# Score tiles of up to 512 columns in a fused attention and FFN kernel, with a few changed places in its schedule

## Chip, cores and metric

The kernel runs on one core of one Trainium2 chip. The metric is device microseconds for one execution; lower is better. Before the change the median of three runs is 322.86 us (322.22 to 323.26).

## What is computed

Two stages follow each other. The first is attention over 4 batches, 8 heads, 768 tokens and a head size of 64, in which a query sees only the keys that fall to the same one of 16 clusters. The second is a gated feed-forward network (FFN) on the 3072 tokens, with a model width of 512 and an inner width of 1536.

```python
q_assign = argmax(q_n . c_n); k_assign = argmax(k_n . c_n)
scores = where(q_assign == k_assign, q @ k.T / sqrt(64), -1e9)
attn = softmax(scores) @ v                      # per batch and head
x = attn, heads side by side                    # 3072 x 512
out = (sigmoid(x @ w_gate) * (x @ w_val)) @ w_out
```

## The kernel before

**Attention.** A head's 768 queries and 768 keys are six blocks of 128 each. q and k are split into a high and a low half-precision part (`hl`: `sp`, `hi`, `lo` in the schedule), turned by a transposing DMA or by TensorE (`turn`, `tn`, `tu`; L410), and stand then in the tile `T`. From T come the cluster logits (`lg`; L421, L434), from these VectorE picks the best cluster (`pick`, `pk`; L449 to L469), and the picked clusters are turned (`ot`) and put into 16 rows of T (`hop`, `hp`, `pl`), so that the score matmul adds the mask by itself.

**Score steps.** `head_steps` (L859) cuts a pass of one head into steps. A step is one key block j against three query blocks: one score matmul of 128 x 384 (L893, `do_scores`), one exponential on ScalarE into the tile `es` (L898), and later three matmuls of 128 x 65 with v (AV; L916, `do_av`). `sc` takes one of four PSUM banks of a ring that gates, values, logits and some v sums (`vt`, L341) use too. Batch 0 goes in two rounds: all eight heads for the first three query blocks (6 steps each), then all for the last three. In the later batches the heads of pairs 0 to 2 are passes of 36 blocks (12 steps), and the last pair's two heads go in two rounds of 18 blocks (6 steps). AV of a step is issued three steps behind its scores in batch 0, two behind in the later ones (`LA`).

**FFN beside attention.** When the first or second half of a batch's queries is done, `ffn_block` puts the FFN of these tokens on a queue: 12 times four gate matmuls (L530), a tanh on ScalarE (L536), four value matmuls (L546) and a product on VectorE (L551), then the output matmuls (L684 in batch 0; L821 with VectorE's sums L768 in the later ones, which make two token blocks' products out of seven half-size ones; `product_out`, L744). `ffn_run` (L845) hands out pieces of this queue after each score step, as far as a credit goes; the credit grows by `ns` nanoseconds a step, from the table `SCHED` by batch and quarter of the batch (`ns23`: batch 2, last quarter).

**Order of the work.** It is written out by hand. `SCHED` gives each background piece a time in steps, relative to the step in which its pair of heads begins: `b1p3lg1` is the logits of the second head of pair 3 in batch 1. `run_bg` (L958) issues what has come due, once at a half step and once at a step. `step_no` counts steps from 0 to 384. Each engine executes its instructions in the order of issue. The pieces `vs`, `vu`, `vt` make the sum of v (L330, L336 and L337, L341); where a batch has no entry of its own, it takes those that begin with `b2`.

**Ends of a pass.** `normalise` (L366, L370 to L375) divides by the sum and writes xp on GpSimd (POOL); `turn_x` (L938) turns xp into xTb, the FFN's input, by a transposing DMA (L947) or, for some pairs of batch 0, by TensorE (L944).

**Constants.** An identity matrix (`ident`), the centroids (`cen`, `c2`) and their squares (`sq`) have tiles of their own; `wo` holds w_out, whose second half (`wo[1]`) is loaded during batch 0's second round.

Of the kernel before, what the change touches and what calls it, by code (L numbers as in the profile page):

```python
# [8 lines left out]
FP = mybir.dt.float32  # L9
HP = mybir.dt.float16  # L10
# [84 lines left out]
}  # L95


@with_exitstack
def kernel(
# [13 lines left out]
    B, H, S, D = q.shape  # L113
# [4 lines left out]
    NCH = S // 128  # L118
# [42 lines left out]
    def bank(n=512, dt=FP, name="bank"):  # L161
        return ring.tile([128, n], dt, tag="ring", name=name)
# [49 lines left out]

    cen = const.tile([128, D], FP, name="cen")

# [62 lines left out]

    c2 = const.tile([128, 2, D], FP, name="c2")
    sq = const.tile([128, D], FP, name="sq")
    ss = const.tile([128, 1], FP, name="ss")  # L280
# [578 lines left out]
    def head_steps(b, p, e, halves):  # L859
        t = T[b, 2 * p + e]  # L860
        steps = []
        cuts = [PARTS[c] if b == 0 else (3 * c, 3) for c in halves]
        for j in range(NCH):
            for c, (a, n) in zip(halves, cuts):
                steps.append(dict(
                    b=b, p=p, e=e, nq=sum(z for _, z in cuts), k=t[:, j, :], h0=cuts[0][0],
                    h1=c, q=t[:, 6 + a : 6 + a + n, :], j=j, c0=a - cuts[0][0], n=n,
                ))
        steps[0]["first"] = True
        steps[-1]["last"] = True  # L870
        return steps
# [14 lines left out]
    def do_scores(s):  # L886
        ready(s)
        sc = bank(128 * s["n"], name="sc")
# [4 lines left out]
        PE.matmul(  # L893
            out=sc.rearrange("p (c t) -> p c t", t=128), lhsT=s["k"], rhs=s["q"],
            start=True, stop=True,
        )
        es = esp.tile([128, NB], HP, name="es")[:, 0 : 128 * s["n"]]
        ACT.activation(es, sc, AF.Exp, scale=SCALE)  # L898
        s["es"] = es

    def do_av(s):
# [12 lines left out]
        a0 = nq * e if both else 0  # L914
        for i in range(s["n"]):
            PE.matmul(  # L916
                out=av[:, a0 + s["c0"] + i, :], lhsT=s["es"][:, bass.ts(i, 128)],
                rhs=VA[b, p][:, e, s["j"], :],
                start=(first and i == 0 and a0 == 0),
                stop=(last and i == s["n"] - 1 and (e == 1 or not both)), skip_group_check=True,  # L920
            )
# [607 lines left out]
    for b in range(B):  # L1529
        xT = xtp.tile([128, NDC, S], HP, tag="xTb", name="xTb")  # L1530
        key = min(b, 1)
        for i in range(2 if b else NPT):
            u = BASE[b] + (DONE0[i] if b == 0 else 96 - 12 * halved(b) if i == 0 else 96)
            lag = SCHED.get(f"lag{key}{i}", 8)
            if b == B - 1 and i:
                break
            c0, cn = PARTS[i] if b == 0 else (3 * i, 3)
            for w in range(1 + (cn > 3)):
                z = cn // (1 + (cn > 3))
                at(u + lag, lambda xT=xT, b=b, a=c0 + z * w, n=z: ffn_block(xT, 128 * a, 128 * n, b))  # L1540
        for p, e, c in heads(b):
            for s in head_steps(b, p, e, c):
                s["xT"] = xT
                do_scores(s)
                run_bg(step_no[0] - 0.5)
                pend.append(s)
                r = step_no[0] - BASE[b]
                ns = SCHED.get(f"ns{b}{r // 24}", SCHED.get(f"ns{b}", 500.0))
                ns += SCHED.get(f"nx{step_no[0]}", 0)
# [41 lines left out]
```

## Time and profile before

| what | value |
|---|---|
| median of three runs | 322.86 us |
| the profiled execution, whole | 323.67 us |
| its span | 321.9 us |
| instructions | 9181 |
| granted TensorE clock | 0.999 |
| exponentials of scores | 384 of 128 x 384 |
| score matmuls | 384 of 128 x 384 |
| AV matmuls | 1152 of 128 x 65 |
| gate and value matmuls | 384 and 384 of 128 x 384 |

The profile is of one execution. Its engines are PE (TensorE), PEld (its weight loads, which overlap), DVE (VectorE), ACT (ScalarE), POOL (GpSimd) and SP (the queue that issues most DMAs). A row of the timeline gives the start, the duration, the engine, the line, the operation, out<-in, the shapes, the count, and in brackets how long the engine was idle before it and what ended that. Records of matmuls overlap, as the ends are those of the last column's way out; the distance from start to start says how long one takes. A row of the groups gives busy time, mean duration in ns, and the idle time before.

### The profile page before, as it was taken

What the parts mean: (1) busy time and instruction counts of PE and PEld (TensorE: products, weight loads), DVE (VectorE), ACT (ScalarE), POOL (GpSimd) and SP (SyncE); (2) the same over time, 40 slices, a digit from 0 to 9 for tenths busy, and PEclk for the clock granted to TensorE, in tenths of its full rate; (3) what the DMA queues carried; (4) which work ended last, traced back from release to release, by engine and by line L of the source; (5) the groups of instructions that cost most, each with busy time, mean ns of one, the idle gap of its engine ahead of it and who ended that gap; (6) DMA issues with size and microseconds to landing.
All of it is one profiled execution on the core that took longest, in us unless ns stands there. A gap on an engine that the chain in (4) does not pass through costs nothing.

```text
span 321.9 us, 9181 instructions
## 1 busy us (share of the span) xinstructions
PE 314.6 (98%) x3510; PEld 222.4 (69%) x3510; DVE 224.9 (70%) x598; ACT 231.1 (72%) x521; POOL 108.6 (34%) x145
## 2 busy tenths in 40 slices
PE   7999999999999999999999999999999999999996
PEld 5888666766666666666777687566777688667775
DVE  5799656777787677576878587586767356456666
ACT  6688988787888888877867866778877886332320
POOL 6877464154434365433133333414211111000000
PEclk9999999999999999999999999999999999999999
DMA  7999997738876996978884751942503112200103
GB/s 214 374 256 180 244 171 118 210 75 236 238 113 187 163 238 155 223 172 136 108 219 115 217 113 33 314 110 52 111 2 90 40 26 79 77 2 1 65 2 131
DMA packets 77709, 45.16 MB, mean 140 GB/s; under 512 B 56865, under 2 KB 75105, under 8 KB 77665
## 3 DMA queue, kind: packets, MB, share of 16 engines
q1 hardware_dynamic: 73696, 39.73, 49.7%
q0 software_dynamic: 3680, 4.72, 9.0%
q8 instruction: 27, 0.44, 0.6%
q10 hardware_dynamic: 288, 0.13, 0.2%
q14 instruction: 18, 0.14, 0.2%
HBM read 28.34 MB, written 6.29 MB: 108 GB/s over the span
## 4 chain that ended last, share of the span: by engine, by line
PE 89%; DMA 3%; DVE 3%; issue 2%; POOL 1%; SPq 0%; ACT 0%; POOLq 0%; DVEq 0%
PE g L530 19%; PE v L546 19%; PE sc L893 17%; PE av L916 10%; PE o L821 8%; PE o L684 5%; PE lg L434 2%; PE o_end L594 2%; DMA T<-hl 2%; PE lg L421 1%; PE t_ps L1142 1%; PE o L594 1%; DMA xTb<-xp 1%; PE oh_ps L1202 1%; DMA qraw<-in_q_dram 1%
## 5 line engine op out<-in xcount | busy, mean ns | idle before, releaser
L898 ACT ACTIVATE es<-sc 128x384 f16<-128x384 f32 x384 | 174.3, 492 | 40.6 <-PE sc L893 31.9
L893 PE MATMUL sc<-T 128*128 128x384 f16 x384 | 117.8, 326 | 0.4 <-DVE T L1223 0.4
L916 PEld LDWEIGHTS <-es 128*128 128x128 f16 x1152 | 81.3, 98 | 35.9 <-issue 0.8
L916 PE MATMUL av<-va,es 128*128 128x65 f16 x1152 | 97.6, 194 | 0.0
L551 DVE SCALAR_TENSOR_TENSOR hT<-th,v 128x384 f16<-128x384 f32 x96 | 53.0, 553 | 55.6 <-PE av L916 36.0
L530 PE MATMUL g<-xTb,wg 128*128 128x384 f16 x384 | 78.2, 326 | 0.7 <-DMA xTb<-xp 0.5
L546 PE MATMUL v<-xTb,wv 128*128 128x384 f16 x384 | 78.1, 326 | 0.0
L536 ACT ACTIVATE th<-g 128x384 f32<-128x384 f32 x96 | 47.2, 491 | 35.0 <-PE g L530 15.9
L375 POOL TENSOR_TENSOR xp<-t,rec 128x384 f16<-128x384 f32 (+1 forms) x30 | 21.6, 720 | 101.8 <-DVE rec L372 52.3
L530 PEld LDWEIGHTS <-wg 128*128 128x128 f16 x384 | 37.2, 97 | 19.3 <-issue 0.4
L546 PEld LDWEIGHTS <-wv 128*128 128x128 f16 x384 | 37.4, 98 | 18.6
L893 PEld LDWEIGHTS <-T 128*128 128x128 f16 x384 | 37.1, 97 | 0.6 <-DVE T L1223 0.5
L1459 POOL TENSOR_TENSOR hl<-kraw,hl 128x384 f16<-128x384 f32 x22 | 20.2, 920 | 41.1 <-DVE hl L1458 20.5
L1459 POOL TENSOR_TENSOR hl<-qraw,hl 128x384 f16<-128x384 f32 x22 | 20.9, 950 | 9.8 <-DVE hl L1458 9.8
L768 DVE TENSOR_TENSOR ob<-o,ob 128x256 f32<-128x256 f32 (+1 forms) x35 | 17.8, 523 | 7.6 <-PE o L821 6.8
L370 DVE TENSOR_TENSOR t<-av,sv 128x390 f32<-128x390 f32 (+1 forms) x30 | 14.4, 479 | 9.7 <-PE av L916 7.3
L821 PEld LDWEIGHTS <-sum 128*128 128x128 f16 x168 | 16.4, 98 | 5.2 <-issue 0.8
L684 PE MATMUL o<-wo,hT 128*128 128x512 f16 x72 | 19.9, 379 | 0.0
L821 PE MATMUL o<-wo,hT 128*128 128x256 f16 x126 | 19.8, 272 | 0.0
L449 DVE TENSOR_REDUCE lgs<-lg 128x192 f32<-128x384 f32 x23 | 12.7, 551 | 2.8 <-PE lg L434 2.7
L821 PEld LDWEIGHTS <-hT 128*128 128x128 f16 x126 | 12.2, 97 | 3.4
L322 POOL CAST va<-vraw 128x768 f16<-128x768 f32 x15 | 13.0, 869 | 1.9 <-DMA vraw<-in_v_dram 1.9
(158 smaller groups left out, 340.1 us busy)
## 6 DMA issues: line engine op xcount, KB each, us to landing
vraw<-in_v_dram SPq DMA_DIRECT2D x15, 384.0 KB, 4.9
kraw<-in_k_dram SPq DMA_DIRECT2D x14, 384.0 KB, 4.3
qraw<-in_q_dram SPq DMA_DIRECT2D x12, 384.0 KB, 4.2
out_dram<-ob SPq DMA_DIRECT2D x18, 256.0 KB, 2.4
wg<-in_moe_w_gate_dram POOLq DMA_DIRECT2D x2, 768.0 KB, 9.5
wv<-in_moe_w_val_dram POOLq DMA_DIRECT2D x2, 768.0 KB, 10.3
wo<-in_moe_w_out_dram POOLq DMA_DIRECT2D x2, 768.0 KB, 9.3
T<-ohT SPq DMA_DIRECT2D x44, 24.0 KB, 1.9
```

Source lines behind the costliest of these rows:

```text
L375: (eng or POOL).tensor_tensor(x, t[:, 0:nq, 0:64], bcast(rec[:, 0:nq], 64), ALU.mult)
L530: PE.matmul(out=g[:, 0:n], lhsT=wg[fc // WQ][:, dc, fc % WQ, :], rhs=xT[:, dc, t0 : t0 + n], start=(dc == 0), stop=(dc == NDC - 1),)
L536: ACT.activation(th[:, 0:n], g[:, 0:n], AF.Tanh)
L546: PE.matmul(out=w[:, 0:n], lhsT=wv[fc // WQ][:, dc, fc % WQ, :], rhs=xT[:, dc, t0 : t0 + n], start=(dc == 0), stop=(dc == NDC - 1),)
L551: DVE.scalar_tensor_tensor(HB[b, blk][:, fc, 0:n], st[0][:, 0:n], 1.0, w[:, 0:n], ALU.add, ALU.mult)
L684: PE.matmul(out=o, lhsT=HB[b, blk][:, fc, bass.ts(t, 128)], rhs=wo[fc // WON][:, fc % WON, :], start=(fc == 0), stop=(fc == NFC - 1),)
L768: plus = lambda dst, a, z: DVE.tensor_tensor(dst, a, z, ALU.add)
L821: PE.matmul(out=st[z][:, e], lhsT=a[:, c, :], rhs=rhs[:, c, :], start=start and c + e == 0, stop=c == HF - 1, skip_group_check=True,)
L893: PE.matmul(out=sc.rearrange("p (c t) -> p c t", t=128), lhsT=s["k"], rhs=s["q"], start=True, stop=True,)
L898: ACT.activation(es, sc, AF.Exp, scale=SCALE)
L916: PE.matmul(out=av[:, a0 + s["c0"] + i, :], lhsT=s["es"][:, bass.ts(i, 128)], rhs=VA[b, p][:, e, s["j"], :], start=(first and i == 0 and a ...
L1459: POOL.tensor_tensor(hl[:, :, 64:128], r, hl[:, :, 0:64], ALU.subtract)
```

## The change

A step is no longer always three blocks. `head_steps` lists the (key block, query block) units of a pass and cuts them into tiles: in the first round of batch 0 three at a time as before; in a pass of 36 nine tiles of four; in a pass of 18 three tiles of four and two of three. A tile may reach over two key blocks: then `do_scores` issues two score matmuls into the two parts of one bank, and one exponential over the whole. `do_av` issues one AV matmul for each unit. A tile counts d = n/3 steps: `step_no` and the credit of the FFN queue grow by that, so background pieces keep their places in units of work, but are issued at the tiles' grid.

So that the larger `es` tiles fit, `ident`, `cen`, `c2` and `sq` lie in `wo[1]`, before it is loaded.

In the table, `b1p3lg1` goes from -29 to -28, `ns23` from 491 to 410, and five entries are new for batch 3, which took those of `b2` before: `vs` of pair 0 -30 (-19), `vu` -28 (-17), `vt` -9 (2), and `lg0` and `pk0` of pair 1 -32 (both -39). `END` is not read.

```diff
-    "b1p3lg0": -38.0, "b1p3pk0": -36.5, ... "b1p3lg1": -29, "b1p3pk1": -27.0,
+    "b1p3lg0": -38.0, "b1p3pk0": -36.5, ... "b1p3lg1": -28, "b1p3pk1": -27.0,
-    "ns21": 491, "ns22": 481, "ns23": 491, "ns30": 443,
+    "ns21": 491, "ns22": 481, "ns23": 410, "ns30": 443,
+    "b3p0vs": -30, "b3p0vu": -28, "b3p0vt": -9, "b3p1lg0": -32, "b3p1pk0": -32, "END": 0,
...
-    NB = 128 * max([3] + SIZES)
+    NB = 512
...
-    ident = const.tile([128, 128], FP, name="ident")
+    spare = wo[1].rearrange("p a m -> p (a m)").bitcast(FP)
+    ident = spare[:, 0:128]
...
-        for j in range(NCH):
-            for c, (a, n) in zip(halves, cuts):
-                steps.append(dict(... k=t[:, j, :], q=t[:, 6 + a : 6 + a + n, :], j=j, n=n))
+        units = [(j, a + z) for j in range(NCH) for a, n in cuts for z in range(n)]
+        if b == 0 and base["h0"] == 0:
+            sizes = [3] * NCH
+        else:
+            sizes = [4] * 9 if len(units) == 36 else [4, 4, 4, 3, 3]
+        for n in sizes:
+            w = []
+            for j, a in units[:n]:
+                if w and w[-1][0] == j:
+                    w[-1] = (j, w[-1][1], w[-1][2] + 1)
+                else:
+                    w.append((j, a, 1))
+            units = units[n:]
+            steps.append(dict(base, w=w, d=n / 3))
...
-        PE.matmul(out=sc..., lhsT=s["k"], rhs=s["q"], start=True, stop=True)
+        for j, a, n in s["w"]:
+            PE.matmul(
+                out=sc[:, x : x + 128 * n].rearrange("p (c t) -> p c t", t=128),
+                lhsT=s["t"][:, j, :], rhs=s["t"][:, 6 + a : 6 + a + n, :], start=True, stop=True,
+            )
+            x += 128 * n
...
-                step_no[0] += 1
+                u = round(3 * (step_no[0] + s["d"])) / 3
+                step_no[0] = int(u) if u == int(u) else u
```

More of the change, by code (lines that the diff above doesn't have):

```diff
@@ L211, in load @@
         eng.dma_start(out=t, in_=view(side, b, p))
-    cen = const.tile([128, D], FP, name="cen")
+    cen = spare[:, 128 : 128 + D]
     def load_head(eng, side, p, e, c=slice(0, 6)):
@@ L276, in mix_wo @@
         DVE.tensor_tensor(o[:, c], a[:, c], z[:, c], ALU.subtract)
-    c2 = const.tile([128, 2, D], FP, name="c2")
-    sq = const.tile([128, D], FP, name="sq")
+    c2 = spare[:, 256 : 256 + 2 * D].rearrange("p (a d) -> p a d", a=2)
+    sq = spare[:, 512 : 512 + D]
     ss = const.tile([128, 1], FP, name="ss")
@@ L862, in head_steps @@
         cuts = [PARTS[c] if b == 0 else (3 * c, 3) for c in halves]
-        for j in range(NCH):
-            for c, (a, n) in zip(halves, cuts):
[L865 to L868, printed above, removed]
+        base = dict(
+            b=b, p=p, e=e, nq=sum(n for _, n in cuts), h0=cuts[0][0], h1=halves[-1], t=t, d=1.0,
+        )
[13 more added lines that the diff above has]
+            steps.append(dict(base, w=w, d=n / 3))
         steps[0]["first"] = True
@@ L887, in do_scores @@
         ready(s)
-        sc = bank(128 * s["n"], name="sc")
+        N = 128 * sum(n for _, _, n in s["w"])
+        sc = bank(N, name="sc")
         for _ in range(SCHED.get(f"nd{step_no[0]}", 0)):
@@ L892, in do_scores @@
             )
[L893 to L897, printed above, removed]
+        x = 0
+        for j, a, n in s["w"]:
+            PE.matmul(
+                out=sc[:, x : x + 128 * n].rearrange("p (c t) -> p c t", t=128),
+                lhsT=s["t"][:, j, :], rhs=s["t"][:, 6 + a : 6 + a + n, :], start=True, stop=True,
+            )
+            x += 128 * n
+        es = esp.tile([128, NB], HP, name="es")[:, 0:N]
         ACT.activation(es, sc, AF.Exp, scale=SCALE)
@@ L914, in do_av @@
         a0 = nq * e if both else 0
-        for i in range(s["n"]):
+        parts = [(j, a + z - s["h0"]) for j, a, n in s["w"] for z in range(n)]
+        for i, (j, c) in enumerate(parts):
             PE.matmul(
-                out=av[:, a0 + s["c0"] + i, :], lhsT=s["es"][:, bass.ts(i, 128)],
-                rhs=VA[b, p][:, e, s["j"], :],
+                out=av[:, a0 + c, :], lhsT=s["es"][:, bass.ts(i, 128)], rhs=VA[b, p][:, e, j, :],
                 start=(first and i == 0 and a0 == 0),
-                stop=(last and i == s["n"] - 1 and (e == 1 or not both)), skip_group_check=True,
+                stop=(last and i == len(parts) - 1 and (e == 1 or not both)),
+                skip_group_check=True,
             )
@@ L1547 @@
                 r = step_no[0] - BASE[b]
[L1548 to L1549 removed]
+                ns = s["d"] * SCHED.get(f"ns{b}{int(r // 24)}", SCHED.get(f"ns{b}", 500.0))
                 ffn_run(ns if b or r >= DONE0[0] else 0.0)
```

4 rows, old and new, of the table SCHED are left out of this document.

## The prediction

> **What bounds the kernel now.** I read the page's table of engines first, then the costliest groups, then stretches of the timeline for TensorE's own spacing, and last the places where TensorE starts late. Page, engines and two groups:
>
> ```profile
> PE 314.6 (98%) x3510; PEld 222.4 (69%) x3510; DVE 224.9 (70%) x598; ACT 231.1 (72%) x521; POOL 108.6 (34%) x145
> ...
> L898 ACT ACTIVATE es<-sc 128x384 f16<-128x384 f32 x384 | 174.3, 492 | 40.6 <-PE sc L893 31.9
> ...
> L536 ACT ACTIVATE th<-g 128x384 f32<-128x384 f32 x96 | 47.2, 491 | 35.0 <-PE g L530 15.9
> ```
>
> TensorE is busy for 98% of the span and every other engine for 72% or less. Busy is not the same as at peak, so here are neighbouring starts on TensorE, from three stretches of its timeline (start, duration, instruction):
>
> ```profile
> 67.81 0.50 PE L1025 MATMUL t_ps<-identh,hl 128*128 128x128 f16 x6
> 68.14 1.03 PE L684 MATMUL o<-wo,hT 128*128 128x512 f16 x4
> 69.00 0.26 PE L916 MATMUL av<-va,es 128*128 128x65 f16 x3
> 69.09 0.33 PE L893 MATMUL sc<-T 128*128 128x384 f16 x1
> ...
> 85.18 0.81 PE L546 MATMUL v<-xTb,wv 128*128 128x384 f16 x4
> 85.83 0.26 PE L916 MATMUL av<-va,es 128*128 128x65 f16 x3
> ...
> 153.81 0.49 PE L821 MATMUL o<-wo,hT 128*128 128x256 f16 x3
> 154.14 0.26 PE L916 MATMUL av<-va,es 128*128 128x65 f16 x3
> ```
>
> Start to start, a matmul of 512 columns takes (69.00 - 68.14)/4 = 0.215 us, of 384 (85.83 - 85.18)/4 = 0.1625, of 256 0.33/3 = 0.11, of 128 0.33/6 = 0.055, three AV matmuls 0.09. The records are longer than that because they overlap. That is 0.42 ns for each column, at 128 columns as at 512, so TensorE streams columns without gaps and is the bound nearly everywhere. The time can fall only where TensorE starts late.
>
> **TensorE's work.** A pass of 36 blocks (one head, all queries) is 12 score matmuls of 384 columns before, 12 x 0.1625 = 1.95 us, and after it six of 512 and six of 256, 6 x (0.215 + 0.11) = 1.95. Nothing is gained. A pass of 18 blocks was six of 384, 0.975 us, and becomes four of 384, two of 256 and two of 128: 0.65 + 0.22 + 0.11 = 0.98. There are 20 such passes (8 in the second round of batch 0, 4 in each later batch), 40 more matmuls in all. The columns are the same; rounding apart, an extra matmul costs some 2 ns. I charge **+0.2 us** for all of it. The lower bound is 0. The upper bound is a 128-column piece that doesn't cover the next weight load. The weight loads' own row:
>
> ```profile
> L893 PEld LDWEIGHTS <-T 128*128 128x128 f16 x384 | 37.1, 97 | 0.6 <-DVE T L1223 0.5
> ```
>
> A load of 97 ns wholly in the open, where 55 ns are paid now, adds 40 x 42 ns = 1.7 us. The six transposes at 67.81 each load weights too and still follow each other in 55 ns, so I stay at the low end.
>
> The Trainium skill, "TensorE: Matmul & The Clock Gate", section "Back-to-back issue gap", says that in a stream of weight load and matmul pairs 128 columns take about 81 ns and not the 56 ns of the isolated formula. By it the 40 pieces would cost an estimated 40 x 26 ns = 1.0 us. The row at 67.81, a stream of just such pairs, shows 55 ns and speaks against it.
>
> **ScalarE's work.** Exponentials go from 384 of 384 columns to 88 of 384 and 222 of 512, 310 in all. The nearest row for 512 columns (groups by form), and a row of exponentials in a chain (timeline):
>
> ```profile
> L694 ACT ACTIVATE ob<-o 128x512 f32<-128x512 f32 x4 | 2.4, 601 | 0.2
> ...
> 32.51 6.52 ACT L898 ACTIVATE es<-sc 128x384 f16<-128x384 f32 x16
> ```
>
> In a chain one exponential follows the last after (6.52 - 0.492)/15 = 0.402 us. One of 512 columns lasts 601 instead of 492 ns, so I take 0.402 + 0.109 = 0.511 (bounds 0.402 and 0.601). Twelve of the old cost 4.82 us, nine of the new 4.60. ScalarE saves about 5 us in all, but it is idle for 28% of the span, so this pays only where TensorE waits for it.
>
> **Where TensorE starts late after the first round, and what becomes of it.** Up to the second round of batch 0 the order of instructions is unchanged, and I count nothing there; the constants that move into the second half of wo are used up long before that half is loaded.
>
> (a) Start of the second round, where scores come with no FFN between them; TensorE's timeline:
>
> ```profile
> 36.52 0.33 PE L893 MATMUL sc<-T 128*128 128x384 f16 x1
> 36.79 0.27 PE L916 MATMUL av<-va,es 128*128 128x65 f16 x3
> ...
> 37.36 0.25 PE L916 MATMUL av<-va,es 128*128 128x65 f16 x3
> 37.55 0.32 PE L893 MATMUL sc<-T 128*128 128x384 f16 x1
> ...
> 38.10 0.33 PE L1297 MATMUL oh_ps<-identh,oh 128*128 128x128 f16 x3
> 38.54 0.34 PE L944 MATMUL x_ps<-identh,xp 128*128 128x128 f16 x3
> ```
>
> Lost against the spacing above: 0.11 at 36.79 and 0.10 at 37.55, both during ScalarE's chain of 16, and 0.27 at 38.54, which waits for POOL's xp. With tiles of four blocks TensorE runs three tiles ahead as before, but that is 12 blocks, not 9, and ScalarE is 5% faster. The first two go; of the third about half stays. Gain 0.35, between 0 and 0.48.
>
> (b) Logits for batch 1's last head that wait for the transposed T (timeline, then the chain's row of the DMA):
>
> ```profile
> 99.02 0.26 PE L916 MATMUL av<-va,es 128*128 128x65 f16 x3
> 99.41 0.47 PE L434 MATMUL lg<-cm,T 128*128 128x32 f16 x12
> ...
> 94.51 4.85 DMA T<-hl
> ```
>
> Lost: 99.41 - 99.02 - 0.09 = 0.30. These are lg1 of b1p3, moved from -29 to -28. In the changed order there are 8.8 us of TensorE work, not 8.1, between its split and its logits, and 0.7 covers 0.30. Gain 0.3.
>
> (c) End of the product of batch 1 (timeline, VectorE and TensorE):
>
> ```profile
> 193.52 0.55 DVE L449 TENSOR_REDUCE lgs<-lg 128x192 f32<-128x384 f32 x1
> 194.10 0.35 DVE L460 TENSOR_REDUCE mx<-lgs 128x12 f32<-128x192 f32 x1
> 194.49 0.43 DVE L462 TENSOR_TENSOR oh<-lgs,mx 128x96 f16<-128x96 f32 x2
> 194.68 0.49 PE L821 MATMUL o<-vheld,sum 128*128 128x256 f16 x3
> 194.95 0.19 DVE L469 TENSOR_SCALAR oh<-oh 128x96 f16<-128x96 f16 x1
> 195.05 1.88 DVE L768 TENSOR_TENSOR ob<-o,ob 128x512 f32<-128x512 f32 x3
> 195.78 0.49 PE L821 MATMUL o<-wo,sum 128*128 128x256 f16 x3 [0.62 <-DVE ob L768]
> ```
>
> The first of the three L768 must empty bank y before TensorE goes on. It stands behind one pick, 1.53 us of VectorE. Lost: 195.78 - 194.68 - 0.33 = 0.77. That pick is pk0 of b3p1, which goes from -39 to -32. In the changed order it stands behind these three L768, in front of one that no matmul waits for soon; the three sums of v of b3p0 leave the place as well. Gain 0.77. If another pick came before an L768, it would stay 0.77.
>
> (d) First gate of batch 2 (timeline, then the chain's row):
>
> ```profile
> 200.48 0.65 PE L530 MATMUL g<-xTb,wg 128*128 128x384 f16 x3
> 201.68 0.32 PE L530 MATMUL g<-xTb,wg 128*128 128x384 f16 x1 [0.54 <-DMA xTb<-xp]
> ...
> 198.06 3.58 DMA xTb<-xp
> ```
>
> Lost: 201.68 - 200.48 - 3 x 0.1625 = 0.71. With ns23 at 410 the FFN queue runs slower in that quarter. From the transposition's place in the order to the first gate there are 5.60 us of TensorE work instead of 4.25; 1.35 more covers 0.71. Gain 0.71. The FFN work left over (1.3 us at the end of attention) runs on TensorE later with nothing waiting, at no cost.
>
> (e) A gate that waits for a bank (timeline):
>
> ```profile
> 206.70 0.22 PE L341 MATMUL vs_ps<-vs,ones 128*128 128x130 f16 x1
> 206.88 0.55 DVE L551 SCALAR_TENSOR_TENSOR hT<-th,v 128x384 f16<-128x384 f32 x1 [0.24 <-PE av L916]
> 207.01 0.32 PE L893 MATMUL sc<-T 128*128 128x384 f16 x1
> 207.49 0.81 PE L530 MATMUL g<-xTb,wg 128*128 128x384 f16 x4
> ```
>
> Lost: 207.49 - 207.01 - 0.1625 = 0.32. The v sum (vt of b3p0) takes one of the four ring banks, so the gate gets the bank that L551 holds until 207.43. With -9 that sum is issued during the product, when only scores use the ring. Gain 0.32.
>
> Sum of gains: 0.35 + 0.3 + 0.77 + 0.71 + 0.32 = 2.45.
>
> **New waits.** Background work now falls on steps 4/3 as far apart, so it comes in larger lumps. The tightest place that I found is the first gate of batch 1:
>
> ```profile
> 125.62 1.25 SPq L947 DMA_TRANSPOSE xTb<-xp  x1
> 128.73 0.81 PE L530 MATMUL g<-xTb,wg 128*128 128x384 f16 x4
> ...
> xTb<-xp SPq DMA_TRANSPOSE x17, 2.5
> ```
>
> Landing at about 125.62 + 2.5 = 128.12, the fourth matmul at 128.73 + 0.49 = 129.22: 1.1 us to spare, of which the new order takes 0.8 (4.74 us of work between the two instead of 5.55). With the 3.58 of (d) it would be late by 3.58 - 2.5 - 0.3 = 0.8. For this and the lumps on VectorE I charge 0.3, between 0 and 1.6 (two waits of the size of (c)).
>
> Sum: -2.45 + 0.2 + 0.3 = -1.95 us. The profiled execution took 323.67 us (span 321.9 and 1.8 around it), 0.8 over the median of 322.86; the same difference is taken from the median: **320.9 us**.
>
> **Rivals.** *All late starts go and no new one comes*: (a) gives 0.48, so -2.58 + 0.2 = -2.4, 320.5; it lies within the forecast's own range, 320.0 to 321.8. *The waits only move*: another DMA or pick takes the place of (c) and (d); then (a), (b) and (e) give 0.97, 0.5 is paid (0.2 and 0.3), 322.4. For it: VectorE is 70% busy, in lumps of 1.5 us. Against it: both have their cover counted in the order. *The small pieces cost their weight load*: 1.7 instead of 0.2, 322.4; against it stands the row at 67.81. By the skill's 81 ns it would be 321.7. *Slower*: each exponential keeps ScalarE 0.109 us longer, each of the 84 gates beside attention (96 less the last block's 12) has its tanh behind one, and its bank and VectorE's product follow late. At full price 84 x 0.109 = 9.2 us, 330; at half of the gates 4.6, 325.5. It decides from 0.023 us a gate (1.95/84). Against it: ScalarE stands idle 35.0/96 = 0.36 us before a tanh on average, the ring turns over more slowly with fewer score tiles, and even now hardly a gate waits. That the tiles don't come about is no rival: the built order shows them.
>
> **How the numbers follow.** Forecast 0.67 (all gains included), moved waits 0.16, small pieces 0.08, slower 0.09. About 0.3% (0.97 us) is what a measurement can tell from no change. Faster holds the forecast and a share of the two cases at 322.4: 0.74; within 0.3%: 0.17; slower: 0.09. The range reaches from 319.8 (320.5, less 0.5 for the spread of the runs, 322.22 to 323.26, and 0.2 for late starts too small to list) to 322.6, past the two cases at 322.4.
>
> **What would show it.** (c), (d) and (e) gone from the places where the product of batch 1 ends and batch 2's FFN begins; TensorE's busy sum within 2 us of 314.6; score matmuls of 128 columns 55 ns ahead of the next start; exponentials of 512 columns near 601 ns, ScalarE's busy time lower by some 5 us. I am wrong if gates wait more often for L551, if the first gate of batch 1 waits for xTb, or if 128-column pieces hold up the next matmul.

## The result and the profile after

| | before | after |
|---|---|---|
| median of eight runs | 322.88 us (322.22 to 323.59) | 325.50 us (323.79 to 326.69) |
| profiled execution, whole and span | 323.67, 321.9 us | 325.86, 323.9 us |

The ratio after to before is 1.0071 (95% 1.0051 to 1.0092): slower by 0.7%, where 0.6% faster was forecast. The granted clock is 1.0, so the loss isn't one of speed. The page of the changed kernel, table of engines and the first row of the chain that ended last:

```profile
PE 314.0 (97%) x3550; PEld 222.9 (69%) x3550; DVE 226.9 (70%) x598; ACT 225.7 (70%) x447; POOL 109.9 (34%) x145
...
PE 84%; DMA 5%; DVE 5%; ACT 2%; POOL 1%; issue 1%; SPq 1%; ACTq 0%; POOLq 0%; DVEq 0%
```

The same row of the chain before:

```profile
PE 89%; DMA 3%; DVE 3%; issue 2%; POOL 1%; SPq 0%; ACT 0%; POOLq 0%; DVEq 0%
```

TensorE's work is the same to 0.6 us, ScalarE has 5.4 us less. But the chain passes through DMAs and VectorE for 10% of the span instead of 6%: TensorE waits more often. Start to start, over all matmuls of the timeline: the 40 more matmuls add 0.2 us, late starts 1.6 net (2.9 more between 40 and 200 us, 1.2 fewer behind that, 0.1 fewer before), and the time behind the last matmul 0.25. Together 2.06, the difference of the spans.

**The forecast gains came.** TensorE's timeline after, where the product of batch 1 ends and batch 2's FFN begins:

```profile
199.18 0.82 PE L823 MATMUL o<-wo,sum 128*128 128x256 f16 x6
199.84 0.29 PE L934 MATMUL av<-va,es 128*128 128x65 f16 x4
...
203.94 0.81 PE L532 MATMUL g<-xTb,wg 128*128 128x384 f16 x4
204.59 0.28 PE L934 MATMUL av<-va,es 128*128 128x65 f16 x4
```

(199.84 - 199.18)/6 = 0.11 and (204.59 - 203.94)/4 = 0.1625 are the bare spacings: the 0.77 of (c) and the 0.71 of (d) are gone, as are (b) and (e).

**New late starts outweigh them.** They begin in the second round of batch 0, in small pieces. TensorE's timeline after:

```profile
45.29 0.30 PE L436 MATMUL lg<-cm,T 128*128 128x32 f16 x6
45.65 0.81 PE L532 MATMUL g<-xTb,wg 128*128 128x384 f16 x4
...
66.37 0.33 PE L909 MATMUL sc<-T 128*128 128x384 f16 x1
66.76 1.02 PE L686 MATMUL o<-wo,hT 128*128 128x512 f16 x4
...
77.65 0.29 PE L934 MATMUL av<-va,es 128*128 128x65 f16 x4
78.03 0.34 PE L962 MATMUL x_ps<-identh,xp 128*128 128x128 f16 x3
```

Six logits take 0.15, so the gate at 45.65 is 0.21 late; the output at 66.76 (waiting for ScalarE's copy into T) lost 0.22, the turn at 78.03 (for POOL's xp) 0.26. With five more such places up to 88 us it is 1.45 us. Then come single larger waits. The first can be followed back through four engines. Timeline after, rows of each engine:

```profile
82.65 0.75 PE L423 MATMUL lg<-cm,T 128*128 128x16 f16 x24
83.44 0.36 DVE L462 TENSOR_REDUCE mx<-lg 128x12 f32<-128x192 f32 x1 [1.47 <-PE lg L423]
...
99.27 0.98 DVE L1476 CAST hl<-kraw 128x384 f16<-128x384 f32 x1
100.63 0.88 DVE L1476 CAST hl<-qraw 128x384 f16<-128x384 f32 x1
101.59 0.92 POOL L1477 TENSOR_TENSOR hl<-qraw,hl 128x384 f16<-128x384 f32 x1 [0.30 <-DVE hl L1476]
102.53 2.16 SPq L412 DMA_TRANSPOSE T<-hl  x1
...
109.09 0.28 PE L934 MATMUL av<-va,es 128*128 128x65 f16 x4
110.48 0.47 PE L436 MATMUL lg<-cm,T 128*128 128x32 f16 x12 [1.11 <-DMA T<-hl]
```

The same instructions before:

```profile
80.85 0.75 PE L421 MATMUL lg<-cm,T 128*128 128x16 f16 x24
81.64 0.36 DVE L460 TENSOR_REDUCE mx<-lg 128x12 f32<-128x192 f32 x1 [1.68 <-PE lg L421]
...
97.52 0.52 DVE L1458 CAST hl<-kraw 128x384 f16<-128x384 f32 x1
99.51 0.35 DVE L1458 CAST hl<-qraw 128x384 f16<-128x384 f32 x1
99.94 0.91 POOL L1459 TENSOR_TENSOR hl<-qraw,hl 128x384 f16<-128x384 f32 x1 [0.85 <-DVE hl L1458]
101.16 2.19 SPq L410 DMA_TRANSPOSE T<-hl  x1
...
108.35 0.45 PE L434 MATMUL lg<-cm,T 128*128 128x32 f16 x12
```

Read it from the top. A set of logits is issued 1.8 us later. VectorE, in order, stands idle until it comes; all that is queued behind the pick moves by the same 1.8, down to a transposing DMA at 88.96 (87.16 before). Further on, VectorE begins a pair's casts 1.75 us later (99.27 against 97.52). Before, it stood idle for 1.0 us between the two casts. This reserve is used up now, since the casts last 0.98 and 0.88 us instead of 0.52 and 0.35: POOL works beside three of the four, and each of these three ends 0.22 us behind POOL's instruction. So POOL's low part ends 1.66 us later, at 102.51, and the transposition at 102.53 starts right behind it, 1.37 later than before. TensorE itself comes only 0.86 later to the next logits (109.09 + 0.12 against 108.35), so 0.5 of the lateness counts. The larger part is the flight, which grew from 6.2 to 7.9 us. Before, the transposed T had landed 1.0 us ahead of the logits; now they start 1.27 after TensorE is ready (110.48 - 109.09 - 0.12). In both kernels the same three loads stand just ahead of this transposition in SP's queue, so these alone don't explain the longer flight; what does stays open.

The second is the place that the prediction named as tightest, the first gate of batch 1. Timeline after:

```profile
127.64 1.19 SPq L965 DMA_TRANSPOSE xTb<-xp  x1
...
130.59 0.65 PE L532 MATMUL g<-xTb,wg 128*128 128x384 f16 x3
131.61 0.32 PE L532 MATMUL g<-xTb,wg 128*128 128x384 f16 x1 [0.37 <-DMA xTb<-xp]
```

Lost: 131.61 - 130.59 - 3 x 0.1625 = 0.53. Here the issue is hardly nearer to the fourth gate than before (3.44 us ahead of it, 3.60 before); it is the flight that grew, from 2.4 to 3.9 us. The third is VectorE itself. Timeline after, VectorE and TensorE:

```profile
175.40 0.81 PE L548 MATMUL v<-xTb,wv 128*128 128x384 f16 x4
175.97 0.41 DVE L770 TENSOR_TENSOR ob<-o,ob 128x256 f32<-128x256 f32 x1
176.30 0.54 DVE L332 TENSOR_TENSOR va<-vraw 128x384 f32<-128x384 f32 x1
...
177.20 0.30 DVE L339 TENSOR_TENSOR vs<-va,va 128x128 f16<-128x128 f32 x1
177.41 0.55 DVE L553 SCALAR_TENSOR_TENSOR hT<-th,v 128x384 f16<-128x384 f32 x1
178.01 0.81 PE L532 MATMUL g<-xTb,wg 128*128 128x384 f16 x4 [0.49 <-DVE hT L553]
```

and the same place before:

```profile
172.51 0.55 DVE L330 TENSOR_TENSOR va<-vraw 128x384 f32<-128x384 f32 x1
...
172.91 0.81 PE L546 MATMUL v<-xTb,wv 128*128 128x384 f16 x4
...
173.83 0.55 DVE L551 SCALAR_TENSOR_TENSOR hT<-th,v 128x384 f16<-128x384 f32 x1
```

The values end at about 176.2, but their product starts at 177.41. The same sums of v (b2p3's, whose entry is unchanged) stand in front of it in both kernels; before, VectorE began them 0.4 us ahead of the value matmuls, now 0.9 behind. The next gate needs the product's bank and is 0.66 late. A bracket is shorter than such a figure, since it counts from the end of the last record, and records overlap; from start to start all new late starts over 60 ns behind 40 us add up to some 4.3 us, against 2.6 that went: the 2.1 of (b) to (e) and six of 0.06 to 0.12 that the prediction didn't list.

### The profile page after: what moved, and what is told of

Same layout as the page of the kernel before. It is cut to its first block, busy times and chain, and to the rows that moved or that the text cites. A ratio compares the mean times of both kernels' runs of the same rounds, so it can differ in the third digit from the quotient of the medians.

```text
span 323.9 us, 9181 instructions
## 1 busy us (share of the span) xinstructions
PE 314.0 (97%) x3550; PEld 222.9 (69%) x3550; DVE 226.9 (70%) x598; ACT 225.7 (70%) x447; POOL 109.9 (34%) x145
## 4 chain that ended last, share of the span: by engine, by line
PE 84%; DMA 5%; DVE 5%; ACT 2%; POOL 1%; issue 1%; SPq 1%; ACTq 0%; POOLq 0%; DVEq 0%
PE v L548 18%; PE g L532 18%; PE sc L909 16%; PE o L823 10%; PE av L934 9%; PE o L686 4%; DMA T<-hl 2%; PE lg L436 2%; DMA kraw<-in_k_dram 2%; PE o_end L596 2%; PE o L596 1%; DMA xTb<-xp 1%; ACT es L915 1%; POOL hl L1139 1%; PE lg L423 1%
## 5 line engine op out<-in xcount | busy, mean ns | idle before, releaser
L915 ACT ACTIVATE es<-sc 128x512 f16<-128x512 f32 (+1 forms) x310 | 169.1, 568 | 50.2 <-PE sc L909 46.3
L909 PE MATMUL sc<-T 128*128 128x256 f16 (+3 forms) x424 | 110.7, 311 | 0.8 <-DVE T L1241 0.4
L934 PEld LDWEIGHTS <-es 128*128 128x128 f16 x1152 | 74.2, 98 | 31.5 <-issue 0.6
L934 PE MATMUL av<-va,es 128*128 128x65 f16 x1152 | 85.7, 193 | 0.0
L538 ACT ACTIVATE th<-g 128x384 f32<-128x384 f32 x96 | 47.2, 492 | 32.1 <-PE g L532 13.7
L909 PEld LDWEIGHTS <-T 128*128 128x128 f16 x424 | 33.6, 97 | 1.5 <-DVE T L1241 0.8
L324 POOL CAST va<-vraw 128x768 f16<-128x768 f32 x15 | 13.7, 915 | 2.9 <-DMA vraw<-in_v_dram 2.9
```

The lines of the kernel that those rows point to most:

```text
L538: ACT.activation(th[:, 0:n], g[:, 0:n], AF.Tanh)
L909: PE.matmul(out=sc[:, x : x + 128 * n].rearrange("p (c t) -> p c t", t=128), lhsT=s["t"][:, j, :], rhs=s["t"][:, 6 + a : 6 + a + n, :], st ...
L934: PE.matmul(out=av[:, a0 + c, :], lhsT=s["es"][:, bass.ts(i, 128)], rhs=VA[b, p][:, e, j, :], start=(first and i == 0 and a0 == 0), stop=( ...
```

## The experiments

Each is told by its edit to the kernel before or to the changed one; times are medians beside runs of the kernel before on the same chip.

**First, the parts.** Threes with the new table entries; tiles of four with the old table; the constants' places alone; and the old tiles with each score matmul in two pieces.

```diff
# e1_table, from before: only these
+  "b1p3lg1": -28, "ns23": 410, "b3p0vs": -30, "b3p0vu": -28, "b3p0vt": -9, "b3p1lg0": -32, "b3p1pk0": -32
# e2_tiles: the changed kernel with the table of before
# e3_alias: from before, ident, cen, c2, sq in wo[1], and NB = 512
# e4_pieces, from before:
-        PE.matmul(out=sc..., lhsT=s["k"], rhs=s["q"], start=True, stop=True)
+        for x, z in ((0, 1), (1, 3)):
+            PE.matmul(out=sc[:, 128 * x : 128 * z]..., lhsT=s["k"], rhs=s["q"][:, x:z], ...)
```

> The kernel before with the seven table entries of the change alone, tiles of three as before. Theory (larger tiles move the background pieces and so make new waits; the table entries keep their gains): the waits of 0.77, 0.71 and 0.32 us at 196, 202 and 207 us and most of the 0.30 at 99 us go, 321.2 us (320.7 to 322.0). Rival (the table entries themselves make the new waits, as ns23 and the moved sums collide with other work): 323.5 us or more.

> The changed kernel with the old table: tiles of four and the shared constants alone. Theory (tiles make the new waits): 325.5 plus the 1.8 us that the table gains, 327.3 us (326 to 328.5). Rival (the table makes them): 322.5 us or less.

> The kernel before with the constants moved into the second half of wo and es tiles of 512 columns of which 384 are used: the places in memory alone. Both theories of the tiles: 322.9 us (322.5 to 323.3), no change. Rival (the places of tiles in memory, or waits on the shared wo tile in the lead-in, slow the first 15 us): 323.8 us or more, with the first AV matmul over 0.5 us later.

> The kernel before with each score matmul cut into one of 128 and one of 256 columns into the same bank, 384 matmuls more and nothing else. Theory (an extra matmul costs the 2 ns of its start): 384 x 2 ns = 0.8 us, 323.7 us (323.3 to 324.3). Rival (a piece of 128 columns doesn't cover the next weight load, 42 ns each): 16 us more, 339 us.

| kernel | us (before 323.18) | ratio (95%) |
|---|---|---|
| e1_table | 322.13 | 0.9963 (0.9949 to 0.9977) |
| e2_tiles | 326.72 | 1.0105 (1.0081 to 1.0128) |
| e3_alias | 323.35 | 1.0001 (0.9985 to 1.0016) |
| e4_pieces | 323.89 | 1.0017 (1.0004 to 1.0030) |

The table alone gains 1.05 to 1.2 us, the tiles alone cost 3.5, and 3.5 - 1.05 is about the 2.6 of the change. The memory places do nothing. The chain row of e1_table's page and the engines' row of e4_pieces' page:

```profile
PE 95%; DVE 2%; ACT 1%; issue 0%; ACTq 0%; POOL 0%; DVEq 0%
```

```profile
PE 314.7 (98%) x3894; PEld 243.1 (75%) x3894; DVE 224.8 (70%) x598; ACT 231.0 (72%) x521; POOL 109.0 (34%) x145
```

With threes and the new table no DMA is left in the chain. In e4_pieces 384 more matmuls cost 0.55 us (0.0017 of 323.2), 1.4 ns each, and TensorE's busy sum stays: small pieces are no cause.

**Second, three mechanisms of the tiles.** That AV now lags two tiles, which is eight blocks and not six (T1); that background comes on a coarser grid (T2); that tanh waits behind longer exponentials (T3). e5_fine issues the background at the old grid's times, e6_avlag keeps AV six (batch 0: nine) blocks behind by cutting tiles, e7_both does both, and e8_la3 keeps threes and lets AV lag nine blocks in all batches.

```diff
# e5_fine, from the changed kernel
-                run_bg(step_no[0] - 0.5)
+                run_bg(step_no[0] - 0.5 + (s["d"] - 1) / 2)
-                run_bg(step_no[0])
+                run_bg(step_no[0] + s["d"] - 1)
# e6_avlag, from the changed kernel (av_run: issues AV block by block, all but the last so many)
-                while len(pend) > LA[min(b, 1)]:
-                    do_av(pend.pop(0))
+                av_run(3 * LA[min(b, 1)])
# e8_la3, from e1_table
-    "la1": 2
+    "la1": 3
```

> The changed kernel, 325.5 us, with the background issued up to the old grid: after a tile of d steps all that was due d - 1 steps later is issued too, half of that after the scores, so that no piece is issued later in units of work than before. Theory T2 (the grid of 4/3 steps issues background late, and the transposing DMAs behind it): 323 us or less. T1 (AV is held back by 8 units instead of 6, so passes end later and xp, xTb and the DMAs queued behind them come late): no more than 0.7 us gained. T3 (the longer exponentials hold up tanh, and so the ring's banks): no change, 325.5.

> The changed kernel with AV held back by 6 units of 128 x 128 in the later batches and by 9 in batch 0, as before, instead of 8 and 12: a tile's AV matmuls are split where needed. T1: 323.5 us or less. T2 and T3: 325 to 326, or longer where AV now waits for the exponential of the tile just ahead (0.6 us each, up to some of the 18 passes).

> Both: background up to the old grid and AV held back by 6 and 9 units. T1 or T2 alone or together: 322 us, near the table entries alone (322.1), since only the number and length of the exponentials are left of the tiles. T3: 325 us or more.

> The kernel before with the new table entries (322.1 us) and AV held back by three tiles of three in the later batches too (9 units instead of 6); tiles and grid as before. T1: 324 us or more, as the dose is larger than the change's 8. T2 and T3: 322.1, no change (321.6 to 322.6).

| kernel | us (before 322.99) | ratio (95%) |
|---|---|---|
| e5_fine | 326.07 | 1.0088 (1.0063 to 1.0113) |
| e6_avlag | 326.53 | 1.0100 (1.0076 to 1.0124) |
| e7_both | 325.93 | 1.0075 (1.0049 to 1.0100) |
| e8_la3 | 324.74 | 1.0048 (1.0033 to 1.0064) |

Neither mend, nor both together, brings anything back: T1 and T2 fall as single causes. The small late starts between 45 and 88 us are still 1.4 us in e7_both; what makes them stays open. The waits behind them only change place. TensorE's timeline in e5_fine, and in e7_both:

```profile
131.08 0.32 PE L532 MATMUL g<-xTb,wg 128*128 128x384 f16 x1 [1.29 <-DMA xTb<-xp]
```

```profile
111.14 0.47 PE L436 MATMUL lg<-cm,T 128*128 128x32 f16 x12 [1.30 <-DMA T<-hl]
```

In e5_fine the wait at the logits is gone and the one for xTb grew to 1.45 from start to start; in e7_both the logits wait 1.46 and xTb 0.76. T3 got the number that it expected of e7_both, but not by its mechanism. The groups of the changed kernel by form:

```profile
L915 ACT ACTIVATE es<-sc 128x512 f16<-128x512 f32 x222 | 129.9, 598 | 41.0 <-PE sc L909 38.6 <-PE vs_ps L343 0.7
L538 ACT ACTIVATE th<-g 128x384 f32<-128x384 f32 x96 | 47.2, 492 | 32.1 <-PE g L532 13.7 <-DVE hT L553 9.7 <-DVE ob L770 4.4
```

The exponentials last the 598 ns that were assumed, and ScalarE still stands idle 32.1/96 = 0.33 us before a tanh, as before (0.36): it waits for gates, not gates for it. Over the 84 gates beside attention, a tanh starts 0.05 us behind its gate's last record on average in both kernels (0.6 at most), and no product on VectorE starts less than 0.15 us after its tanh has ended, so none waits for it. What grew is the time from the last value matmul to the product, from 0.14 to 0.23 us on average: VectorE comes to it later. e8_la3 is worth more than its own verdict: with threes and the good table, a later AV alone costs 2.8 us (+1.75 against -1.05, each beside its own before), as T1 expected, though taking the lag away from the tiles of four brought nothing. Here too the cost is waits for landings (1.54 us late at a set of logits at 123.06). Almost any delay costs the same kind of time here.

**Third, where the lateness comes from.** Either it arises wherever tiles of four make pieces late on VectorE, batch 0's second round first, and is handed on (V), with its rival that each batch makes its own; or what decides is when the split and turn of T are issued, whoever is late (D). e9_late4 has threes in all of batch 0 and fours behind it; e10_first4 has fours only in batch 0's second round. In e11_lead all splits and turns (`sp`, `tn`) come two steps earlier; in e12_late, on e1_table, one step later.

```diff
# e9_late4, from the changed kernel
-        if b == 0 and base["h0"] == 0:
+        if b == 0:
# e10_first4, from the changed kernel
-        if b == 0 and base["h0"] == 0:
-            sizes = [3] * NCH
+        if b or base["h0"] == 0:
+            sizes = [3] * (len(units) // 3)
# e11_lead, from the changed kernel, with ns13 235 instead of 265; e12_late, from e1_table: + 1
-            at(use + o, g)
+            at(use + o - (2 if name[:2] in ("sp", "tn") else 0), g)
```

> The changed kernel with tiles of three in all of batch 0, tiles of four in batches 1 to 3 alone. Theory V (a piece that comes late on an engine makes VectorE, which works in order, late; GpSimd, the transposing DMAs and the logits follow, and the lateness that reaches batch 1 begins in batch 0): with nothing late at unit 96 the waits of 1.3 and 0.5 us at 110 and 131 us shrink, 323.7 us (322.8 to 324.6). Rival W (each stage loses by its own tiles, nothing is handed on): only the 1.0 us lost up to unit 96 goes, 324.5 us or more.

> Tiles of four in the second round of batch 0 alone, threes in batches 1 to 3, new table. V: the lateness of batch 0 is handed on and costs again at the logits and the first gate of batch 1, 324 us (323.2 to 325). W: 322.1 of the table alone plus the 1.0 us of that round, 323.1 us or less.

> The changed kernel with splits and transposing DMAs of batches 1 to 3 two steps earlier (about 1.3 us) and the FFN's pace in the last quarter of batch 1 at 235 instead of 265. Theory D (the cost is transposing DMAs that land after TensorE wants them): the waits at 110 us (1.27) and 131 us (0.54) go, 323.7 us (323 to 324.5). Rival (VectorE's order is the cost, and earlier splits are only another disturbance of it): 325 us or more, with new waits for VectorE.

> The kernel before with the new table (322.1 us), tiles of three, and splits and transposing DMAs of batches 1 to 3 one step later (about 0.7 us). Theory D: the four logits groups that had 0 to 1 us to spare at 99 to 126 us wait up to 0.6 us each, 323.5 us (322.8 to 324.5). Rival (DMAs have spare time, only larger tiles hurt): 322.1 us, no change.

| kernel | us (before 323.12) | ratio (95%) |
|---|---|---|
| e9_late4 | 323.60 | 1.0008 (0.9990 to 1.0026) |
| e10_first4 | 324.24 | 1.0036 (1.0023 to 1.0050) |
| e11_lead | 327.75 | 1.0128 (1.0100 to 1.0157) |
| e12_late | 323.71 | 1.0019 (1.0007 to 1.0032) |

Against its before, e1_table stands at -1.05, e9_late4 at +0.5, e10_first4 at +1.1, the change at +2.6. So fours in batch 0's second round cost 2.2 us (e10 less e1; 2.1 by the change less e9), fours behind it 1.5 (e9 less e1; 1.5 by the change less e10). The two parts add up to the whole, 3.7. Where the 2.2 are lost shows e10_first4, in which everything from batch 1 on is in threes; TensorE's timeline:

```profile
122.74 0.47 PE L436 MATMUL lg<-cm,T 128*128 128x32 f16 x12 [0.40 <-DMA T<-hl]
```

The tiles here are those of before, yet the T of these logits lands 0.56 late, xTb 0.55 late at 131.3, and hT's bank 0.57 at 177.6; before, none of the three places lost as much as 0.06. The lateness of 45 to 82 us is handed on. So both kernels stand at theory V's numbers (324 and 323.7), and its rival's are missed. How far the lateness reaches shows the T of the logits that start at 110.48 in the changed kernel and at 109.52 here (e10_first4, SP's timeline and TensorE's):

```profile
102.58 1.97 SPq L412 DMA_TRANSPOSE T<-hl  x1
...
109.52 0.45 PE L436 MATMUL lg<-cm,T 128*128 128x32 f16 x12
```

It is issued as late as in the changed kernel (102.53), while e9_late4 (101.33) and e1_table (101.17) stand near the kernel before: this lateness does come from batch 0. But T flies 6.1 us here, and its logits don't wait. In the kernels with the three loads ahead of it, it flew 7.5 to 7.9 us where these logits wait 1.2 to 1.5 us (the changed kernel, e2_tiles, e6_avlag, e7_both), and 5.7 to 6.5 where they don't. So the lateness alone doesn't make the wait; it takes the longer flight as well.

In e9_late4 the waits at 110 and 131 us are gone and another one has come, 0.93 from start to start; TensorE's timeline:

```profile
121.46 0.47 PE L436 MATMUL lg<-cm,T 128*128 128x32 f16 x12 [0.77 <-DMA T<-hl]
```

e11_lead missed its expectation by 4 us: a remedy that creates its own wait. The waits of 1.27 and 0.53 are gone, as theory D said, but scores wait 0.55 at 107.31 and logits 0.89 at 126.83 in their place, and the largest loss comes early. Two steps earlier, the T of one pair goes ahead of others in SP's queue, which TensorE needs first (TensorE's timeline, 54 to 57 us):

```profile
55.04 0.24 PE L436 MATMUL lg<-cm,T 128*128 128x32 f16 x3 [0.55 <-DMA T<-hl]
56.85 0.24 PE L436 MATMUL lg<-cm,T 128*128 128x32 f16 x3 [1.57 <-DMA T<-hl]
```

That is 2.4 us from start to start, and in the profiled execution a slower clock behind it (below). e12_late came out near its expectation, 1.6 us over e1_table, but by luck: the logits that theory D named wait no longer than in e1_table (0.15 at 100.73). What costs is one wait of 0.88 us at 58.54 for POOL's hl, and a gate 0.53 late at 176.29: the same kind of chain, at other links.

**Fourth, first mends.** e13_lead2 is e11_lead with only the pairs from b1p2 on moved, so that the trouble at 55 us stays away. e14_mend is e9_late4 with b2p1's splits and turns two steps earlier and b3p0's v sums three later.

```diff
# e13_lead2, from the changed kernel, with ns13 235
+            at(use + o - (2 if name[:2] in ("sp", "tn") and (b > 1 or p > 1) else 0), g)
# e14_mend, from e9_late4, with "b3p0vs": -27, "b3p0vu": -25
+            at(use + o - (2 if name[:2] in ("sp", "tn") and (b, p) == (2, 1) else 0), g)
```

> As the run with all leads, but the splits and transposing DMAs of batch 1's pair 1 stay where they are in the changed kernel; those of pairs 2 and 3 of batch 1 and of batches 2 and 3 are two steps earlier, and the FFN's pace in the last quarter of batch 1 is 235. Theory D (late DMAs are most of the cost after batch 0): from 325.5 the waits at 110 us (1.27) and 131 us (0.54) go and the early stall of that run does not come, 323.7 us (323.0 to 324.5). Rival (any move of a piece costs, wherever it goes): 325.5 us or more.

> The changed kernel with tiles of three in batch 0 (323.6 us), the splits and DMAs of batch 2's pair 1 two steps earlier, and the first sums of v for batch 3 at -27 and -25 instead of -30 and -28. Theory (what was left was one late DMA, 0.93 us at 121 us, and VectorE behind a sum of v, 0.77 us at 176 us): 321.9 us (321.2 to 322.8), at or below the table alone (322.1). Rival (the waits only move on): 323.3 us or more.

e13_lead2: 325.80 us beside 323.61, ratio 1.0077 (1.0049 to 1.0105). e14_mend: 323.68, ratio 1.0003 (0.9991 to 1.0015). Neither is better than what it mends; both stand at their rivals' numbers. In e13_lead2 the waits at 110 and 178 us are gone; in their place scores wait 0.88 for the picked clusters (T<-ohT), and later logits, at 123.38, 1.16 for T. e14_mend was partly misaimed: the sums of v that stand at 175 us are b2p3's, and not those that it moved, so the wait there stayed (0.48). The logits' wait stayed too, 0.77 of 0.93.

**Last, single places.** Three kernels that swap what stands in front of a late piece and leave TensorE's order as it was. e15_loads puts b2p1's three raw loads behind the transposition of T that stood behind them (102.53 in the changed kernel), and nothing else. e16_mend3 is e9_late4 with b2p2's load of v behind the T of the late logits, and with the right sums of v earlier. e17_mend4 does all three in the changed kernel.

```diff
# e15_loads, from the changed kernel
+  "b2p1lk": 9.5, "b2p1lq": 9.5, "b2p1lv": 9.5
# e16_mend3, from e9_late4
+  "b2p2lv": 9.5, "b2p3vs": -23, "b2p3vu": -21
# e17_mend4, from the changed kernel: both
```

> The changed kernel with one swap on SP's queue and nothing else: the three raw loads of b2p1 are issued right behind the transposition of T that stood behind them (102.53 us in the changed kernel) and not ahead of it. If the 1.27 us late logits at 110.48 come from SP's in-order queue, that transposition starts near 100.8, lands before 109.2, the wait there is below 0.2, and the time is 324.3 (by 1.2 below the changed kernel's 325.5) if nothing else takes its place. Rival, the waits move on: the wait is gone but the time stays at 325 or more, with the gate at 131.6 or logits near 122 later by as much. Second rival, the flight and not the queue decides: the transposition starts early, but lands no earlier than 110 since the loads share the DMA engines, and the wait stays at 1 us or more.

> Threes in batch 0, fours behind it, with two swaps: the load of v of b2p2 goes behind the transposition of T at 114.75 us (whose logits are 0.93 late at 121.46), and the sums of v of b2p3, which stand in front of the late hT at 175.00, come earlier (-23 and -21 for -19 and -17), ahead of a block of output sums. If these two places are what is left of the cost of the later fours: 321.9 to 322.3 (323.6 less 0.93 and 0.76, with 0.3 of doubt), the wait near 175.6 below 0.1. Rival, waits move on: 323.3 or more. If only the v sums help: 322.9.

> The changed kernel with all swaps of the two kernels above (b2p1's loads and b2p2's load of v behind the transposition of T that stood behind them, v sums of b2p3 earlier). If each wait is a place of its own: 325.5 less 1.2 less 0.8 is 323.5, and fours in batch 0's second round keep costing the 1.4 us of small late starts between 45 and 88 us. Rival, lateness is handed on whatever is mended: 325 or more.

| kernel | us (before 323.39) | ratio (95%) |
|---|---|---|
| e15_loads | 327.23 | 1.0104 (1.0065 to 1.0143) |
| e16_mend3 | 322.81 | 0.9981 (0.9963 to 0.9999) |
| e17_mend4 | 325.19 | 1.0048 (1.0031 to 1.0065) |

e15_loads is the cleanest. Its timeline, SP and TensorE:

```profile
102.24 1.42 SPq L412 DMA_TRANSPOSE T<-hl  x1
...
108.92 0.46 PE L436 MATMUL lg<-cm,T 128*128 128x32 f16 x12
...
123.92 0.47 PE L436 MATMUL lg<-cm,T 128*128 128x32 f16 x12 [1.75 <-DMA T<-hl]
```

The transposition starts 0.3 us earlier in its trace, but so does all of TensorE's work since the first round (the scores at 37.43 in the changed kernel start at 37.16 here). It doesn't wait for the queue: POOL's low part ends at 102.21 here, 0.03 ahead of it. So the expected earlier start, 100.8, didn't come. Yet T lands after 3.3 us instead of 7.9. With the loads behind it and not ahead, the DMA engines are busy for 0.31 of the time from 102 to 104 us, against 0.91 in the changed kernel. The wait of 1.27 us is gone, and TensorE is 1.28 us ahead of the changed kernel there. So that wait does hang on the place in SP's queue, but by the flight behind the loads and not by the start. But the loads now stand ahead of the next transpositions, which fly 5.8 and 7.5 us: logits at 114.2, 123.9 and the gate at 132.7 are 0.39, 1.91 and 0.89 late. The median is above the changed kernel's, though the six executions spread from 324.76 to 328.88 and the intervals overlap; that nothing is gained is what they show. The rival "waits move on" holds, by transfers that the trace shows.

e16_mend3 is the first kernel with tiles of four that beats the one before, at the edge of its interval. T has 3.3 us of flight instead of 6.7 and its logits wait no more; the gate behind the product of values is 0.22 late instead of 0.48. One wait has come, and with it the time missed the expected 321.9 to 322.3. TensorE's timeline:

```profile
129.49 0.32 PE L532 MATMUL g<-xTb,wg 128*128 128x384 f16 x1 [0.96 <-DMA xTb<-xp]
```

That is 1.12 us for the xTb that the prediction had named; it flew 4.1 us here and 2.4 in the kernel before. e17_mend4 came out at its rival's 325: it gains 0.8 on the changed kernel (+1.8 beside its before, against +2.6) and not 2.0. The small late starts of 45 to 88 us are all there, 1.45 us, and behind them logits at 122.9 and the gate at 131.5 wait 0.64 and 0.78.

The best version run stays e1_table, 322.13 us, faster than both kernels. Open is whether an order can be found in which tiles of four cost nothing; the waits at 110 and 121 us could each be removed by a swap and that at 175 halved, but another transfer took part of the place each time.

## Why the prediction was wrong

- **TensorE's work, +0.2**: right. By the spacings it is 0.23, and e4_pieces puts an extra piece at 1.4 ns instead of the 2 assumed. The 81 ns that the Trainium skill, "TensorE: Matmul & The Clock Gate", section "Back-to-back issue gap", gives for a stream of pairs would have made e4_pieces 384 x 26 ns = 10 us slower by estimate; 0.55 was measured.
- **ScalarE**: right, 5.4 us less (some 5 forecast), 598 ns for 512 columns (601), and no gain from it, as said.
- **(b), (c), (d), (e), 2.1 together**: right as mechanisms; all four late starts are gone. e1_table, which has (b) to (e) by the table alone, gains 1.05 to 1.2 of the 2.1, and its trace shows where the rest went: (b) keeps 0.16 of its 0.30, and logits at 126.3, values at 184.1 and a gate at 217.9 are 0.16, 0.23 and 0.37 late, which they weren't before. That is 0.92, and leaves 1.2.
- **(a), 0.35**: mis-sized; 0.2 was gained. Between 36 and 39 us 0.62 was lost before (the three places, and 0.13 at 37.94 that the prediction didn't list) and 0.42 after: the wait for xp went, but the scores, whose waits were to go, still start late (0.07 at 37.43, 0.21 at 37.92).
- **"New waits: I charge 0.3, between 0 and 1.6"**: this step failed. 4.3 us were measured, far beyond the upper bound. The prediction counted the slack of each landing in TensorE's work between two instructions of the order, as if the transfer were issued where the order says and flew as long as before. Neither held. A transfer is issued when VectorE, POOL and SP come to it, each in order: T was issued 1.37 us later at 102.53, the product of values at 177.41 is late by VectorE alone, and the small late starts from 45 to 88 us, which the prediction only calls lumps on VectorE, cost 1.45. And the flight isn't fixed: that T flew 6.2, 7.9 and 3.3 us in the kernel before, the changed one and e15_loads, xTb 2.4 and 3.9 before and after. At both places the longer flight (1.7 and 1.5 us) is more than what was lost (1.27 and 0.53). The tightest place was named rightly, and so was its condition, a flight like the 3.58 of (d); but logits that weren't looked at cost more.
- **"Slower"** as a rival gave 325.5, the time that came, but by tanh behind longer exponentials, which the traces speak against (tanh starts as soon behind its gate as before). Its number was right by luck. "The waits only move" was nearer in mechanism, with a price for two places instead of a dozen.

Shown by the runs: the split of the loss (2.2 for batch 0's second round, 1.5 for the later fours, -1.05 for the table); that lateness made in batch 0 turns up in batches 1 and 2; that the wait at 110.48 hangs on the flight of T behind the loads (e15_loads) and part of that at 178.01 on the sums in front (e16_mend3); that pieces, memory places, AV's lag and the grid, alone or together, don't carry the loss, and, by the traces, tanh doesn't. Only argued, from traces: that the logits issued 1.8 us late at 82.65 are the start of the lateness at 102.53. Open: what makes the small late starts of batch 0's second round, and what lengthened the flights of T and xTb where the queue ahead was the same.

## What to carry to other kernels

In a kernel whose bound engine is 98% busy, a regrouping of its work is priced at the hand-overs: for each transfer and each in-order queue, list the slack at its consumer before the change, and ask how late the issuer can become, not only how much work lies between. Ask the same of the flight: here a small transposition took 3.3 us with the loads behind it and 5.7 to 7.9 with them ahead, and with a microsecond to spare it decided whether a late issue was absorbed or became a wait. Test the parts apart: here the small part of the change was worth taking, and the large one cost three times as much.

## What the runs showed of the hardware

In the profiled execution of e11_lead two idle stretches of TensorE (0.72 and 1.72 us, within 2.5 us) were followed by half the clock. The windows of that kernel (stretch, its length, busy time of PE, PEld, DVE, ACT and POOL, granted clock, DMA share, GB/s), and one row of its timeline:

```profile
54.00:58.00 4.00, 1.88 (x24) 1.16 (x22) 0.87 (x3) 1.27 (x4) 0.91 (x1) 0.99 0.21 34
58.00:61.00 3.00, 3.00 (x18) 1.82 (x17) 2.67 (x6) 1.54 (x4) 2.16 (x3) 0.50 0.04 9
```

```profile
58.42 1.49 PE L548 MATMUL v<-xTb,wv 128*128 128x384 f16 x4
59.70 0.43 PE L934 MATMUL av<-va,es 128*128 128x65 f16 x4
```

A matmul of 384 columns takes (59.70 - 58.42)/4 = 0.32 us there, twice the 0.1625. The half clock lasts from 57.9 to about 61.3, some 3.4 us, which cost about 1.7 us of columns (half of it). The Trainium skill, "TensorE: Matmul & The Clock Gate", section "What's actually happening", puts the fall to half the clock behind an idle window of about 3.4 us. The length of the slow stretch agrees with such a window; the idle time doesn't, as neither gap was longer than 1.72 us and both together 2.44. Single gaps of 1.3 us (the changed kernel at 110) and 1.9 us (e15_loads at 122) left the clock at 1.0 in their profiled executions. So the two waits of 2.4 us and the half clock behind them cost some 4 in this execution. They don't in each one: of the six executions of e11_lead two have a mean granted clock of 0.995 (328.49 and 327.13 us), and one at 1.0 took 328.36, so the half clock isn't what makes this kernel slow. Nor is it bound to these waits: the profiled execution of e6_avlag has 3.4 us of half clock from 11.9 us on, in the first round, whose order is that of the kernel before.
